# One-bank PSUM tiles in place of two-bank tiles in a fused linear-attention and token-MLP block

## The chip, the cores and the metric

The kernel runs on one core of one Trainium2 chip. The time is the device time of the execution in microseconds (us), the median of several runs; lower is better. Each run also has a mean granted TensorE clock, where 1.0 is full speed.

## The reference, cut to what matters

With x of 2048 rows and 576 columns, 32 heads of 18, and an MLP over the *rows* (tokens) with 4608 hidden units, the reference computes:

```
q, k, v = layernorm(x) @ wqkv                       # 576 -> 3 x 576
pq, pk  = phi(q), phi(k)                            # phi(t) = t+1 if t > 0 else exp(t); + 1e-6
kv, z   = pk^T v, sum over rows of pk               # per head: the "state"
o       = (pq kv) / (pq z + 1e-6)
h       = x + o @ wo
u       = gelu(layernorm(h)^T @ w1 + b1)            # contraction over 2048 rows
out     = h + (u @ w2 + b2)^T
```

Inputs and output are bf16; sums are taken in f32.

## The kernel before

It works on 16 tiles of 128 rows. It has three stages.

1. *Projections and state.* Each row tile is normalised, transposed on TensorE and evicted by ScalarE (ACT); K comes in two halves of 288 columns, V in two parts, and the state is accumulated over all tiles. After every four row tiles a "Q block" computes five groups of Q for 512 rows.
2. *Attention output, projection, second normalisation.* `nd` is the attention output of a row tile; it is divided on VectorE (DVE), transposed by a DMA into `oT`, and projected into `at`. ScalarE copies `at` to `h` with a sum and squares it with a sum; GpSimd (POOL) writes the normalised `hn`. The attention outputs run LOOK tiles ahead of the projection.
3. *The MLP.* Blocks `u` and `y`, 1152 matmuls of 288 columns each.

The program uses PSUM, the memory that matmuls write to, as eight banks of 512 f32 columns. Before, it is handed out in tiles of two banks, and four such tiles exist. One is held by the state (`kvz`) during stage 1, so three rotate.

```python
    ps = ctx.enter_context(tc.tile_pool(name="ps", bufs=4, space=bass.MemoryType.PSUM))
    def acc_tile(name):
        return ps.tile([P, 2, BANK], F32, tag="acc", name=name)

        def phi_evac(ps_ap, out_ap, rows, cols):       # exp on ACT, max on DVE, + eps on POOL
            e = ...
            nc.scalar.activation(out=e, in_=ps_ap, func=ACT.Exp, bias=-1.0, scale=1.0)
            nc.vector.scalar_tensor_tensor(out=m, in0=e, scalar=1.0, in1=ps_ap, op0=ALU.min, op1=ALU.max)
            nc.gpsimd.tensor_scalar(out=out_ap, in0=m, scalar1=1.0, scalar2=PHI_EPS, ...)

        def emit_q(c):
            for g in range(NG):                        # NG = 5
                if g % 2 == 0:
                    qps = acc_tile(f"qps{c}_{g}")      # groups g and g+1 share a two-bank tile
                reg = qps[:rg, g % 2, 0:SC]
                for kt in range(KT):                   # KT = 5 matmuls of 512 columns
                    nc.tensor.matmul(reg, ...)
                phi_evac(reg, ...)                     # reads this bank before the next group is written
        ...
            # stage 2: one copy of both banks with one sum, then the square with that sum as bias
            nc.scalar.activation(out=h_sb[:, i, :]..., in_=at_ps[:, :, 0:HD], func=ACT.Identity, accum_out=hsum)
            nc.scalar.activation(out=junk, in_=h_sb[:, i, :], func=ACT.Square, bias=hsum, ..., accum_out=ssq)
```

K has the same form as Q: half 0 goes to bank 0 and is evicted by `phi_evac`, then half 1 goes to bank 1 of the same tile. The transposes of a row tile lie in the unused columns of the K tile's two banks, so the K tile is taken from the rotation already at the transposes.

## Time and profile before

The median is 427.44 us over six runs (427.01 to 428.52). The profiled run has a span of 425.8 us at a mean clock of 0.995.

| from the span's start | us |
|---|---|
| first Q block starts | 28.8 |
| starts of the four Q blocks | 28.8, 50.9, 73.2, 98.1 |
| last state matmul starts | 95.8 |
| u starts | 139.4 |
| last u matmul starts | 280.7 |
| last y matmul starts | 421.8 |

The windows view gives, for a stretch of time, each engine's busy time (with the number of instructions), then the granted clock, the share of the DMA engines and the GB/s. The kernel before, with two lines for the first two cycles of stage 1 (a Q block and four row tiles each), one for stage 2 and one for u:

```profile
core 0: us, PE busy (x) PEld busy (x) DVE busy (x) ACT busy (x) POOL busy (x), PEclk, DMA share, GB/s
28.77:50.90 22.13, 18.98 (x146) 13.19 (x145) 12.46 (x33) 11.63 (x35) 8.86 (x18) 1.00 0.37 89
50.90:73.19 22.29, 18.99 (x146) 13.19 (x145) 11.46 (x29) 11.63 (x35) 9.09 (x19) 1.00 0.00 1
...
96.00:139.40 43.40, 37.24 (x298) 27.46 (x298) 25.97 (x95) 28.33 (x69) 27.23 (x50) 0.96 0.38 62
139.40:280.80 141.40, 141.40 (x1155) 112.76 (x1155) 0.41 (x3) 27.24 (x36) 1.86 (x4) 1.00 0.56 146
```

In the MLP TensorE is busy all the time, so nothing is to be had there. In stage 1 no engine is full, and in stage 2 none either: both are chains with waits in them. The waits view (who waited, for whom, us in total, times, longest) of the kernel before, TensorE only; waits at the start of the kernel and short ones are left out:

```profile
...
PE kps L214 <- DVE m L166: 4.5, 6, 1.0
PE qps L262 <- DVE m L166: 4.4, 5, 1.4
PE at L355 <- DMA oT<-o_buf: 3.1, 6, 1.5
PE kps L227 <- DVE m L166: 2.1, 3, 0.9
...
PE bps L404 <- DMA b_raw<-in_B_b_dram: 1.8, 1, 1.8
PE vps L235 <- DVE m L166: 0.9, 4, 0.4
...
```

Four of the six lines shown wait for the same instruction: L166, the maximum in `phi_evac`. They are of two kinds. L227 is K's second half, which waits until the first half's bank has been read. L214 (the transposes) and L235 (V) open a new tile, so they wait for one of the three tiles to come free. The timeline shows how. Its columns are start, duration, engine, line, operation, out<-in, shapes, and in brackets the idle time before and what ended it. This is the third Q block before, from the timelines of TensorE and VectorE:

```profile
73.19 2.32 PE L262 MATMUL qps<-xnT,wqkv_sb 128*126 128x512 bf16 x10
75.97 1.24 PE L262 MATMUL qps<-xnT,wqkv_sb 128*126 128x512 bf16 x5 [0.17 <-DVE m L166]
78.69 2.32 PE L262 MATMUL qps<-xnT,wqkv_sb 128*72 128x512 bf16 x10 [1.37 <-DVE m L166]
...
75.23 0.69 DVE L166 SCALAR_TENSOR_TENSOR m<-e,qps 126x512 f32<-126x512 f32 x1 [2.09 <-ACT e L164]
77.95 1.29 DVE L166 SCALAR_TENSOR_TENSOR m<-e,qps 126x512 f32<-126x512 f32 x2 [2.03 <-ACT e L164]
```

Read it across the engines: the maximum that starts at 75.23 ends at 75.92, and the group that goes to the *other* bank of that tile starts at 75.97. TensorE has put a few other matmuls in between, then runs out of them. The longer wait, 1.37 us before 78.69, is of the other kind: there the fifth group (72 rows) opens a new tile, and the tile that it gets comes free only when its second half has been read too, by the first of the two maxima at 77.95. The fifth group waits 1.37 us in each of the first three Q blocks. Twenty-five matmuls that take 5.4 us back to back (25 x 0.215) are spread over 7.8 us here.

### The profile page before, as it was taken

The numbers are of one execution on the slowest core, as the hardware profiler recorded it, in microseconds if no ns is written. First come the engines' busy times: TensorE is split into PE (matmuls) and PEld (weight loads), VectorE is DVE, ScalarE is ACT, GpSimd is POOL, SyncE is SP. The second block draws the span as 40 slices with busy tenths as digits, with TensorE's granted clock in tenths as the row PEclk, the third lists the DMA queues.
The fourth block names the chain that finished last, engine by engine and source line by source line (L and its number), as shares of the span: only waits on it lengthen the run. The fifth ranks groups of instructions, "written<-read, shape, count | busy, mean of one in ns | idle before, by whom it ended". The sixth has DMA issues, their size and how long they took to land.

```text
span 425.8 us, 7334 instructions
## 1 busy us (share of the span) xinstructions
PE 393.6 (92%) x3158; PEld 303.7 (71%) x3158; DVE 88.1 (21%) x263; ACT 101.5 (24%) x235; POOL 64.9 (15%) x132
## 2 busy tenths in 40 slices
PE   2887979788988999999999999999999999999996
PEld 1554747465765777777777777777777777777774
DVE  4655554326764000000000000000100001000010
ACT  2435545452778311221221122110000000000000
POOL 3333444321778200000000000000000000000000
PEclk9999999998999999999999999999999999999999
DMA  8774000004343997473463553000927639276300
GB/s 247 227 200 97 3 0 2 0 2 48 62 77 63 264 292 189 108 187 103 128 169 100 145 152 100 0 2 15 235 71 196 158 93 236 80 185 170 81 22 21
DMA packets 92687, 48.23 MB, mean 113 GB/s; under 512 B 12528, under 2 KB 92656, under 8 KB 92656
## 3 DMA queue, kind: packets, MB, share of 16 engines
q1 hardware_dynamic: 92656, 47.78, 43.8%
q8 instruction: 24, 0.39, 0.4%
q14 instruction: 7, 0.06, 0.0%
HBM read 42.78 MB, written 2.36 MB: 106 GB/s over the span
## 4 chain that ended last, share of the span: by engine, by line
PE 80%; DVE 8%; DMA 5%; ACT 3%; issue 2%; POOL 1%; SPq 1%; DVEq 0%; ACTq 0%; POOLq 0%
PE u L419 33%; PE y L433 33%; PE qps L262 5%; DVE m L166 4%; PE at L355 3%; DMA oT<-o_buf 3%; PE kps L227 3%; ACT e L164 2%; DVE stats L189 2%; DMA x_sb<-in_A_x_dram 2%; DVE xn_buf L198 1%; PE nd L323 1%; PE vps L235 1%; POOL rstd L196 1%; PE at L352 1%
## 5 line engine op out<-in xcount | busy, mean ns | idle before, releaser
L419 PE MATMUL u<-hn_sb,w1c 128*128 128x288 bf16 x1152 | 141.5, 286 | 0.0
L433 PE MATMUL y<-gT_sb,w2c 128*128 128x288 bf16 x1152 | 141.3, 286 | 0.0
L433 PEld LDWEIGHTS <-w2c 128*128 128x128 bf16 x1152 | 112.7, 98 | 28.4
L419 PEld LDWEIGHTS <-w1c 128*128 128x128 bf16 x1152 | 112.6, 98 | 28.4
L437 DVE SCALAR_TENSOR_TENSOR o_t<-y,b_sb,h_sb 128x576 bf16<-128x576 f32 x16 | 13.1, 818 | 269.3 <-PE y L433 269.3
L422 ACT ACTIVATE gT_sb<-u,b_sb 128x576 bf16<-128x576 f32 x36 | 26.7, 742 | 113.2 <-PE u L419 113.2
L227 PE MATMUL kps<-wqkv_sb,xnT 128*128 128x288 bf16 x160 | 27.3, 295 | 3.9 <-DVE m L166 2.1
L262 PE MATMUL qps<-xnT,wqkv_sb 128*126 128x512 bf16 (+1 forms) x100 | 24.7, 393 | 4.5 <-DVE m L166 4.4
L355 PE MATMUL at<-wo_sb,oT 128*128 128x288 bf16 x160 | 24.6, 286 | 3.1 <-DMA oT<-o_buf 3.1
L235 PE MATMUL vps<-wqkv_sb,xnT 128*128 128x378 bf16 (+1 forms) x160 | 25.3, 295 | 0.9 <-DVE m L166 0.9
L262 PEld LDWEIGHTS <-wqkv_sb 128*126 128x126 bf16 (+1 forms) x100 | 13.6, 137 | 12.7 <-issue 6.1
L227 PEld LDWEIGHTS <-xnT 128*128 128x128 bf16 x160 | 15.3, 100 | 8.8 <-issue 4.6
L235 PEld LDWEIGHTS <-xnT 128*128 128x128 bf16 x160 | 15.6, 101 | 8.2 <-issue 2.7
L355 PEld LDWEIGHTS <-oT 128*128 128x128 bf16 x160 | 14.9, 98 | 8.7 <-DMA oT<-o_buf 4.6
L214 PE MATMUL kps<-ident,xn_buf 128*128 128x128 bf16 x80 | 7.6, 229 | 12.1 <-POOL hm L300 5.5
L168 POOL TENSOR_SCALAR pk_buf<-m 128x288 bf16<-128x288 f32 x32 | 13.9, 434 | 28.1 <-DVE m L166 20.3
L164 ACT ACTIVATE e<-kps 128x288 f32<-128x288 f32 x32 | 13.2, 412 | 18.9 <-PE kps L227 18.5
L166 DVE SCALAR_TENSOR_TENSOR m<-e,qps 126x512 f32<-126x512 f32 (+1 forms) x20 | 13.0, 683 | 22.4 <-ACT e L164 22.4
L164 ACT ACTIVATE e<-qps 126x512 f32<-126x512 f32 (+1 forms) x20 | 11.1, 595 | 26.3 <-PE qps L262 26.3
L166 DVE SCALAR_TENSOR_TENSOR m<-e,kps 128x288 f32<-128x288 f32 x32 | 14.3, 447 | 14.4 <-ACT e L164 14.1
L168 POOL TENSOR_SCALAR pqT_sb<-m 126x512 bf16<-126x512 f32 (+1 forms) x20 | 12.5, 623 | 29.6 <-DVE m L166 28.9
L214 PEld LDWEIGHTS <-xn_buf 128*128 128x128 bf16 x80 | 5.8, 102 | 15.1 <-DVE xn_buf L198 8.1
(63 smaller groups left out, 196.3 us busy)
## 6 DMA issues: line engine op xcount, KB each, us to landing
w1c<-in_B_w_dram SPq DMA_DIRECT2D x18, 1024.0 KB, 6.0
w2c<-in_B_w_dram SPq DMA_DIRECT2D x8, 2304.0 KB, 10.0
out_dram<-o_t SPq DMA_DIRECT2D x16, 144.0 KB, 2.0
wqkv_sb<-in_A_wqkv_dram SPq DMA_DIRECT2D x3, 576.0 KB, 5.2
x_sb<-in_A_x_dram SPq DMA_DIRECT2D x3, 576.0 KB, 8.2
wo_sb<-in_A_wo_dram SPq DMA_DIRECT2D x1, 576.0 KB
x_sb<-in_A_x_dram SPq DMA_DIRECT2D x2, 144.0 KB, 2.1
x_sb<-in_A_x_dram SPq DMA_DIRECT2D x1, 288.0 KB
```

The costliest lines, as they stand in the source:

```text
L164: nc.scalar.activation(out=e[:rows, :cols], in_=ps_ap, func=ACT.Exp, bias=-1.0, scale=1.0)
L166: nc.vector.scalar_tensor_tensor(out=m[:rows, :cols], in0=e[:rows, :cols], scalar=1.0, in1=ps_ap, op0=ALU.min, op1=ALU.max)
L168: nc.gpsimd.tensor_scalar(out=out_ap, in0=m[:rows, :cols], scalar1=1.0, scalar2=PHI_EPS, op0=ALU.mult, op1=ALU.add)
L214: nc.tensor.transpose(dst, xn[:, kt * P:(kt + 1) * P], ident)
L227: nc.tensor.matmul(kps[:, hh, 0:HD], lhsT=xnT[:, kt, ssl], rhs=wqkv_sb[:, kt, WK + hh * HD:WK + (hh + 1) * HD], start=(kt == 0), stop=(kt ...
L235: nc.tensor.matmul(vps[:, b, 0:w], lhsT=xnT[:, kt, ssl], rhs=wqkv_sb[:, kt, WV + c0:WV + c0 + w], start=(kt == 0), stop=(kt == KT - 1))
L262: nc.tensor.matmul(reg, lhsT=wqkv_sb[:, kt, WQ + g_off[g]:WQ + g_off[g] + rg], rhs=xnT[:, kt, :], start=(kt == 0), stop=(kt == KT - 1))
L355: nc.tensor.matmul(at_ps[:, hh, 0:HD], lhsT=oT[:, kt, :], rhs=wo_sb[:, kt, hh * HD:(hh + 1) * HD], start=False, stop=(kt == KT - 1))
L419: nc.tensor.matmul(acc[:, hh, 0:HD], lhsT=w1c[:, k, j * P:(j + 1) * P], rhs=hn_sb[:, k, hh * HD:(hh + 1) * HD], start=(k == 0), stop=(k == ...
L422: nc.scalar.activation(out=gT_sb[:, ft, :].rearrange("p (a b) -> p a b", a=2), in_=acc[:, :, 0:HD], func=ACT.Gelu_apprx_tanh, bias=b1_sb[: ...
L433: nc.tensor.matmul(acc[:, hh, 0:HD], lhsT=w2c[:, ft, j * P:(j + 1) * P], rhs=gT_sb[:, ft, hh * HD:(hh + 1) * HD], start=(ft == 0), stop=(f ...
L437: nc.vector.scalar_tensor_tensor(out=o_t.rearrange("p (a b) -> p a b", a=2), in0=acc[:, :, 0:HD], scalar=b2_sb[:, i:i + 1], in1=h_sb[:, i, ...
```

## The change

The change hands PSUM out in eight tiles of one bank. The state takes two and six rotate in stage 1. It is meant to end the waits that come from the two-bank tile, and it pays for that with more and smaller instructions where one instruction used to read both banks. With it come a separate tile for the five transposes (one eviction of 640 columns instead of two), LOOK 4 with five buffers instead of LOOK 3 with four, and the MLP's bias load moved to the start. The core of the diff:

```diff
-    ps = ctx.enter_context(tc.tile_pool(name="ps", bufs=4, space=bass.MemoryType.PSUM))
-    def acc_tile(name):
-        return ps.tile([P, 2, BANK], F32, tag="acc", name=name)
+    ps = ctx.enter_context(tc.tile_pool(name="ps", bufs=8, space=bass.MemoryType.PSUM))
+    def bank_tile(name):
+        return ps.tile([P, BANK], F32, tag="bank", name=name)
 ... transposes
-            nc.scalar.activation(out=xnT[:, 0:TB0, ssl], in_=tv0, func=ACT.Identity)
-            nc.scalar.activation(out=xnT[:, TB0:KT, ssl], in_=tv1, func=ACT.Identity)
+            nc.scalar.activation(out=xnT[:, :, ic * P:(ic + 1) * P], in_=tv, func=ACT.Identity)
 ... K (V and nd in the same way)
-            kps = k_tiles.pop(i)
             for hh in range(2):
+                kps = bank_tile(f"kps{i}_{hh}")
 ... Q
-                if g % 2 == 0:
-                    qps = acc_tile(f"qps{c}_{g}")
-                reg = qps[:rg, g % 2, 0:SC]
+                qps = bank_tile(f"qps{c}_{g}")
+                reg = qps[:rg, 0:SC]
 ... projection: two copies with a sum each, and an addition of the sums on VectorE
+            for hh in range(2):
+                ...
+                nc.scalar.activation(out=h_sb[:, i, hh * HD:(hh + 1) * HD], in_=at_ps[:, 0:HD],
+                                     func=ACT.Identity, accum_out=hs[:, hh:hh + 1])
-            nc.scalar.activation(out=h_sb[:, i, :]..., in_=at_ps[:, :, 0:HD], func=ACT.Identity, accum_out=hsum)
+            nc.vector.tensor_tensor(out=hsum, in0=hs[:, 0:1], in1=hs[:, 1:2], op=ALU.add)
 ... lookahead (and five o and oT buffers instead of four)
-        LOOK = 3
+        LOOK = 4
 ... MLP: gelu and the last addition in two halves each; b1, b2 loaded and transposed earlier
```

More of the change, by code (lines that the diff above doesn't have):

```diff
@@ L67 @@
     VB = D - VA
-    TB0 = 3
-    assert (BANK - HD) * 2 >= TB0 * P and (BANK - HD) * 2 >= (KT - TB0) * P
     persist = ctx.enter_context(tc.tile_pool(name="persist", bufs=1))
@@ L127 @@
         nc.sync.dma_start(wo_sb[:RLAST, KT - 1, :], A_wo[(KT - 1) * P:D, :])
+        b1_raw = pa.tile([FT, P], BF16)
+        nc.sync.dma_start(b1_raw, B_b1.rearrange("(ft p) -> ft p", p=P))
+        b2_raw = pa.tile([NS, P], BF16)
+        nc.sync.dma_start(b2_raw, B_b2.rearrange("(i p) -> i p", p=P))
         nc.vector.memset(wqkv_sb[RLAST:P, KT - 1, :], 0.0)
@@ L150 @@
             v_bufs.append(vb)
-        NOB = 4
+        NOB = 5
         o_bufs = []
@@ L169, in phi_evac @@
                                     op0=ALU.mult, op1=ALU.add)
-        kvz = acc_tile("kvz")
-        kvz_a = kvz[:, 0, :].rearrange("p (g c) -> p g c", c=P)
-        kvz_b = kvz[:, 1, 0:P]
+        kvz_at = bank_tile("kvz_a")
+        kvz_a = kvz_at.rearrange("p (g c) -> p g c", c=P)
+        kvz_bt = bank_tile("kvz_b")
+        kvz_b = kvz_bt[:, 0:P]
         def kvz_region(g, nrows, c0, c1):
@@ L180 @@
         xnT_tiles = {}
-        k_tiles = {}
         ln_norm = {}
@@ L206, in emit_tr @@
             xn = xn_bufs[i % NXB]
-            kps = acc_tile(f"kps{i}")
-            k_tiles[i] = kps
-            tv = [kps[:, b, HD:BANK].bitcast(BF16) for b in range(2)]
-            tv0 = tv[0][:, 0:TB0 * P].rearrange("p (k c) -> p k c", c=P)
-            tv1 = tv[1][:, 0:(KT - TB0) * P].rearrange("p (k c) -> p k c", c=P)
-            for kt in range(KT):
-                dst = tv0[:, kt, :] if kt < TB0 else tv1[:, kt - TB0, :]
-                nc.tensor.transpose(dst, xn[:, kt * P:(kt + 1) * P], ident)
-            ssl = slice(ic * P, (ic + 1) * P)
-            nc.scalar.activation(out=xnT[:, 0:TB0, ssl], in_=tv0, func=ACT.Identity)
-            nc.scalar.activation(out=xnT[:, TB0:KT, ssl], in_=tv1, func=ACT.Identity)
+            tps = bank_tile(f"tps{i}")
+            tv = tps.bitcast(BF16)[:, 0:KT * P].rearrange("p (k c) -> p k c", c=P)
+            for kt in range(KT):
+                nc.tensor.transpose(tv[:, kt, :], xn[:, kt * P:(kt + 1) * P], ident)
+            nc.scalar.activation(out=xnT[:, :, ic * P:(ic + 1) * P], in_=tv, func=ACT.Identity)
         def emit_kv(i):
@@ L223, in emit_kv @@
             pk_sb = pk_bufs[i % NPK]
-            kps = k_tiles.pop(i)
             for hh in range(2):
+                kps = bank_tile(f"kps{i}_{hh}")
                 for kt in range(KT):
-                    nc.tensor.matmul(kps[:, hh, 0:HD], lhsT=xnT[:, kt, ssl],
+                    nc.tensor.matmul(kps[:, 0:HD], lhsT=xnT[:, kt, ssl],
                                      rhs=wqkv_sb[:, kt, WK + hh * HD:WK + (hh + 1) * HD],
                                      start=(kt == 0), stop=(kt == KT - 1))
-                phi_evac(kps[:, hh, 0:HD], pk_sb[:, hh * HD:(hh + 1) * HD], P, HD)
+                phi_evac(kps[:, 0:HD], pk_sb[:, hh * HD:(hh + 1) * HD], P, HD)
             v_sb = v_bufs[i % NVB]
-            vps = acc_tile(f"vps{i}")
             for b, (c0, w) in enumerate(((0, VA), (VA, VB))):
+                vps = bank_tile(f"vps{i}_{b}")
                 for kt in range(KT):
-                    nc.tensor.matmul(vps[:, b, 0:w], lhsT=xnT[:, kt, ssl],
+                    nc.tensor.matmul(vps[:, 0:w], lhsT=xnT[:, kt, ssl],
                                      rhs=wqkv_sb[:, kt, WV + c0:WV + c0 + w],
                                      start=(kt == 0), stop=(kt == KT - 1))
-            nc.scalar.activation(out=v_sb[:, 0:NPB, 0:RG],
-                                 in_=vps[:, 0, 0:VA].rearrange("p (g c) -> p g c", c=RG), func=ACT.Identity)
-            nc.scalar.activation(out=v_sb[:, NPB, 0:RG], in_=vps[:, 1, 0:RG], func=ACT.Identity)
-            nc.scalar.activation(out=v_sb[:, NPB + 1, 0:VB - RG], in_=vps[:, 1, RG:VB], func=ACT.Identity)
+                if b == 0:
+                    nc.scalar.activation(out=v_sb[:, 0:NPB, 0:RG],
+                                         in_=vps[:, 0:VA].rearrange("p (g c) -> p g c", c=RG), func=ACT.Identity)
+                else:
+                    nc.scalar.activation(out=v_sb[:, NPB, 0:RG], in_=vps[:, 0:RG], func=ACT.Identity)
+                    nc.scalar.activation(out=v_sb[:, NPB + 1, 0:VB - RG], in_=vps[:, RG:VB], func=ACT.Identity)
         def emit_kvacc(i):
@@ L254, in emit_q @@
             xnT = xnT_tiles[c]
-            qps = None
             for g in range(NG):
                 rg = g_rows[g]
-                if g % 2 == 0:
-                    qps = acc_tile(f"qps{c}_{g}")
-                reg = qps[:rg, g % 2, 0:SC]
+                qps = bank_tile(f"qps{c}_{g}")
+                reg = qps[:rg, 0:SC]
                 for kt in range(KT):
@@ L286 @@
         emit_kvacc(NS - 1)
+        bps = bank_tile("bps")
+        bpv = bps.bitcast(BF16)
+        nc.tensor.transpose(bpv[:, 0:FT], b1_raw, ident[:FT, :FT])
+        nc.tensor.transpose(bpv[:, 512:512 + NS], b2_raw, ident[:NS, :NS])
+        nc.vector.tensor_copy(out=b1_sb, in_=bpv[:, 0:FT])
+        nc.vector.tensor_copy(out=b2_sb, in_=bpv[:, 512:512 + NS])
         bm = pa.tile([P, GH, Dh], F32)
@@ L318, in emit_nd @@
         def emit_nd(i):
-            nd = acc_tile(f"nd{i}")
-            for g in range(NG):
-                rg = g_rows[g]
-                b, sl = divmod(g, NPB)
-                nc.tensor.matmul(nd[:, b, sl * NDW:sl * NDW + RG + GH],
-                                 lhsT=pqT_sb[:rg + 1, g, i * P:(i + 1) * P],
-                                 rhs=R_sb[:rg + 1, g, 0:RG + GH], start=True, stop=True)
             rden = small.tile([P, NG, GH], F32, tag="rden")
             o_sb = o_bufs[i % NOB]
+            nds = []
             for b in range(2):
@@ L330, in emit_nd @@
                 g0 = b * NPB
-                ndv = nd[:, b, 0:ns_ * NDW].rearrange("p (s c) -> p s c", c=NDW)
-                nc.vector.reciprocal(out=rden[:, g0:g0 + ns_, :], in_=ndv[:, :, RG:RG + GH])
+                nd = bank_tile(f"nd{i}_{b}")
+                for sl in range(ns_):
+                    g = g0 + sl
+                    rg = g_rows[g]
+                    nc.tensor.matmul(nd[:, sl * NDW:sl * NDW + RG + GH],
+                                     lhsT=pqT_sb[:rg + 1, g, i * P:(i + 1) * P],
+                                     rhs=R_sb[:rg + 1, g, 0:RG + GH], start=True, stop=True)
+                nds.append(nd)
             for b in range(2):
@@ L335, in emit_nd @@
                 g0 = b * NPB
-                ndv = nd[:, b, 0:ns_ * NDW].rearrange("p (s c) -> p s c", c=NDW)
+                ndv = nds[b][:, 0:ns_ * NDW].rearrange("p (s c) -> p s c", c=NDW)
+                nc.vector.reciprocal(out=rden[:, g0:g0 + ns_, :], in_=ndv[:, :, RG:RG + GH])
                 nc.vector.tensor_tensor(
@@ L341, in emit_nd @@
                     op=ALU.mult)
-            oT = work.tile([P, KT, P], BF16, tag="oT", name=f"oT{i}", bufs=4)
+            oT = work.tile([P, KT, P], BF16, tag="oT", name=f"oT{i}", bufs=5)
             nc.sync.dma_start_transpose(out=oT, in_=o_sb)
@@ L349, in emit_wo_h @@
             oT = oT_tiles.pop(i)
-            at_ps = acc_tile(f"at{i}")
+            hs = small.tile([P, 2], F32, tag="hs")
             for hh in range(2):
-                nc.tensor.matmul(at_ps[:, hh, 0:HD], lhsT=ident, rhs=x_sb[:, i, hh * HD:(hh + 1) * HD],
+                at_ps = bank_tile(f"at{i}_{hh}")
+                nc.tensor.matmul(at_ps[:, 0:HD], lhsT=ident, rhs=x_sb[:, i, hh * HD:(hh + 1) * HD],
                                  start=True, stop=False)
                 for kt in range(KT):
-                    nc.tensor.matmul(at_ps[:, hh, 0:HD], lhsT=oT[:, kt, :],
+                    nc.tensor.matmul(at_ps[:, 0:HD], lhsT=oT[:, kt, :],
                                      rhs=wo_sb[:, kt, hh * HD:(hh + 1) * HD],
                                      start=False, stop=(kt == KT - 1))
+                nc.scalar.activation(out=h_sb[:, i, hh * HD:(hh + 1) * HD], in_=at_ps[:, 0:HD],
+                                     func=ACT.Identity, accum_out=hs[:, hh:hh + 1])
             hsum = small.tile([P, 1], F32, tag="hsum")
-            nc.scalar.activation(out=h_sb[:, i, :].rearrange("p (a b) -> p a b", a=2), in_=at_ps[:, :, 0:HD],
-                                 func=ACT.Identity, accum_out=hsum)
+            nc.vector.tensor_tensor(out=hsum, in0=hs[:, 0:1], in1=hs[:, 1:2], op=ALU.add)
             junk = work.tile([P, D], BF16, tag="junk", bufs=2)
@@ L396 @@
         outp = bctx.enter_context(tc.tile_pool(name="outp", bufs=3))
-        b1_raw = pb.tile([FT, P], BF16)
-        nc.sync.dma_start(b1_raw, B_b1.rearrange("(ft p) -> ft p", p=P))
-        b2_raw = pb.tile([NS, P], BF16)
-        nc.sync.dma_start(b2_raw, B_b2.rearrange("(i p) -> i p", p=P))
-        bps = acc_tile("bps")
-        bpv = [bps[:, b, :].bitcast(BF16) for b in range(2)]
-        nc.tensor.transpose(bpv[0][:, 0:FT], b1_raw, ident[:FT, :FT])
-        nc.tensor.transpose(bpv[1][:, 0:NS], b2_raw, ident[:NS, :NS])
-        nc.vector.tensor_copy(out=b1_sb, in_=bpv[0][:, 0:FT])
-        nc.vector.tensor_copy(out=b2_sb, in_=bpv[1][:, 0:NS])
         gT_sb = pb.tile([P, FT, D], BF16)
@@ L415 @@
                 ft = fc * (FCW // P) + j
-                acc = acc_tile(f"u{ft}")
+                accs = [bank_tile(f"u{ft}_{hh}") for hh in range(2)]
                 for k in range(NS):
                     for hh in range(2):
-                        nc.tensor.matmul(acc[:, hh, 0:HD], lhsT=w1c[:, k, j * P:(j + 1) * P],
+                        nc.tensor.matmul(accs[hh][:, 0:HD], lhsT=w1c[:, k, j * P:(j + 1) * P],
                                          rhs=hn_sb[:, k, hh * HD:(hh + 1) * HD],
                                          start=(k == 0), stop=(k == NS - 1))
-                nc.scalar.activation(out=gT_sb[:, ft, :].rearrange("p (a b) -> p a b", a=2), in_=acc[:, :, 0:HD],
-                                     func=ACT.Gelu_apprx_tanh, bias=b1_sb[:, ft:ft + 1], scale=1.0)
+                for hh in range(2):
+                    nc.scalar.activation(out=gT_sb[:, ft, hh * HD:(hh + 1) * HD], in_=accs[hh][:, 0:HD],
+                                         func=ACT.Gelu_apprx_tanh, bias=b1_sb[:, ft:ft + 1], scale=1.0)
         w2v = B_w2.rearrange("(ft p) s -> p ft s", p=P)
@@ L429 @@
                 i = sc * (SCW // P) + j
-                acc = acc_tile(f"y{i}")
+                accs = [bank_tile(f"y{i}_{hh}") for hh in range(2)]
                 for ft in range(FT):
                     for hh in range(2):
-                        nc.tensor.matmul(acc[:, hh, 0:HD], lhsT=w2c[:, ft, j * P:(j + 1) * P],
+                        nc.tensor.matmul(accs[hh][:, 0:HD], lhsT=w2c[:, ft, j * P:(j + 1) * P],
                                          rhs=gT_sb[:, ft, hh * HD:(hh + 1) * HD],
@@ L436 @@
                 o_t = outp.tile([P, D], BF16, tag="o_t")
-                nc.vector.scalar_tensor_tensor(
-                    out=o_t.rearrange("p (a b) -> p a b", a=2), in0=acc[:, :, 0:HD], scalar=b2_sb[:, i:i + 1],
-                    in1=h_sb[:, i, :].rearrange("p (a b) -> p a b", a=2), op0=ALU.add, op1=ALU.add)
+                for hh in range(2):
+                    nc.vector.scalar_tensor_tensor(
+                        out=o_t[:, hh * HD:(hh + 1) * HD], in0=accs[hh][:, 0:HD], scalar=b2_sb[:, i:i + 1],
+                        in1=h_sb[:, i, hh * HD:(hh + 1) * HD], op0=ALU.add, op1=ALU.add)
                 nc.sync.dma_start(out2[i * P:(i + 1) * P, :], o_t)
```

## The prediction

> **What bounds the kernel now.** Three stages, by the windows view. (1) 0 to 96 us: projections and state. (2) 96 to 139.5 us: attention output, projection, second normalisation. (3) 139.5 to 422 us: two MLP matmul blocks of 141 us each with TensorE never waiting; 3.7 us of tail follow. Stage 3 is bound by TensorE and keeps its 1152 + 1152 matmuls at 123 ns, so only stages 1 and 2 (139.5 us) can move.
>
> Stage 1: from the timeline's start-to-start spacing, one row tile costs TensorE about 3.0 us (5 transposes 0.28, ten 288-column matmuls 1.22, V 1.23, state 0.28), one Q block 5.4 us (25 x 0.215). Four tiles plus a Q block are 17.4 us; the trace takes 22.1 to 22.8 us. The waits view names the reason: TensorE waits for the DVE maximum (L166) before kps, qps and vps. The instruction order shows why: each two-bank tile is tracked as one, so the second half's matmuls wait until exp (0.41 to 0.60 us) and maximum (0.45 to 0.69 us) of the first half have read the other bank; only three such tiles rotate.
>
> **What the change does there.** One-bank tiles end the false wait, six banks rotate, and TensorE's new order is plain program order. A bank is needed again five groups later, about 2.7 us, against about 1.4 us of exp + maximum. The two transpose evictions (0.49 + 0.38) become one of 640 columns: 0.72 us by the Trainium skill ("ScalarE: Activation LUTs", What ACT_TABLE_LOAD costs: 186 ns + 0.833 ns per column; the trace agrees, 493 ns at 384). ACT needs about 2.6 and DVE about 2.4 us a tile, both under 3.0. I estimate the first Q block at 24 us (now 28.8; start-up stays held by loads, a slow TensorE and the normalisation chain) and 18.3 us a cycle: the state ends near 80.5 us instead of 96, a gain of about 15.5 us.
>
> **What it costs.** Stage 2: ACT now spends about 1.65 us a tile (copy 0.55, accumulator read 0.22, square 0.68, read 0.2), close to TensorE's 1.77, and tiles pass at about 1.85 us. Afterwards copy and accumulator read come twice (0.53 each), then ACT waits for the new DVE add (about 0.25 with hops), then square 0.88: 2.2 us a tile in order, so ACT becomes the bound. Q3 is no longer interleaved: projection begins about 10 us after the state (6.6 now). hn of tile 15 comes about 47.3 us after the state; u's last k step needs it. Before, u's end lay 185 us after the state; afterwards about 47.3 + 140.9 = 188.2. Loss about 3 us, in spite of the early bias load, which takes away a 1.8 us wait. LOOK 4 and the fifth buffers barely matter once ACT bounds. Gelu in halves (72 x about 0.5 us) stays hidden. The last output addition gains about 0.1 us.
>
> **Predicted.** 427.4 - 15.5 + 3.2 = about 415.3 us; range 410.5 to 421.5. Faster by over 2%: 0.78; within 2%: 0.21; slower: 0.01.
>
> **Right if:** waits of kps, qps, vps on L166 nearly vanish from the waits view; Q blocks lie 18 to 19 us apart; kvz ends at 79 to 83 us; in stage 2 the square waits for the hsum add, tiles pass every 2.1 to 2.4 us; u and y stay 141 us each.
>
> **Wrong if:** six banks or the DVE order (normalisation between maxima) still stall TensorE, cycles 20 us or more; or ACT hides the add, and stage 2 shortens too; or start-up, held by loads, gives nothing.

## The result

The changed kernel takes 403.67 us (median of eight runs, 403.05 to 405.0), the kernel before 427.21 us in the same rounds (16 runs). The ratio is 0.9453, with a 95% interval from 0.9436 to 0.9471: it is 5.5% faster. Among runs at a clock of 0.998 or more the means are 426.3 (runs of before beside the experiments) and 403.7. Here and below a ratio is the mean time of one kernel's fast runs over that of the other's in the same rounds, so it is not quite the ratio of the quoted medians. The direction was right; the time lies below the predicted range (410.5 to 421.5), since the gain is 23.7 us and not 12.

| us | before | after |
|---|---|---|
| span of the profiled run | 425.8 | 402.1 |
| starts of the four Q blocks | 28.8, 50.9, 73.2, 98.1 | 23.6, 41.6, 59.0, 79.8 |
| last state matmul starts | 95.8 | 76.6 |
| first projection matmul starts | 102.6 | 85.2 |
| u starts, last u matmul starts | 139.4, 280.7 | 113.6, 256.6 |
| last state matmul to last u matmul | 184.9 | 180.0 |
| last u matmul to the end of the span | 145.1 | 145.5 |

The gain of 23.7 us is thus 19.2 in stage 1 (95.8 - 76.6), 4.9 from there to the end of u, and -0.4 after it. Two reservations: the profiles of x6 and x13 below, whose stage 1 has the code of before, have the last state matmul at 95.0 and 94.5, so about 1 us of the 19.2 may be scatter of one profile; and some 1.4 to 1.7 of the 4.9 are a dip of the clock in the profile of before ("The clock dip" below). The windows view after, the same four stretches:

```profile
23.61:41.59 17.98, 17.59 (x149) 13.04 (x147) 14.72 (x43) 11.88 (x30) 9.45 (x19) 1.00 0.68 177
41.59:59.02 17.43, 17.43 (x149) 13.05 (x147) 11.84 (x30) 11.88 (x30) 10.15 (x21) 1.00 0.00 1
...
76.70:113.60 36.90, 35.05 (x302) 26.95 (x300) 27.55 (x109) 26.65 (x92) 24.37 (x44) 1.00 0.40 73
113.60:256.80 143.20, 141.49 (x1155) 112.75 (x1153) 0.73 (x5) 35.26 (x81) 4.94 (x10) 1.00 0.54 144
```

In the second cycle TensorE is busy for 17.43 of 17.43 us: stage 1 is now bound by TensorE once it has started. In u, 1.7 us of the 143.2 are idle. The waits view after, TensorE, again without the start:

```profile
...
PE u L415 <- POOL hn_sb L383: 1.7, 2, 1.4
PE kps L224 <- DVE m L169: 1.0, 2, 0.5
PE at L361 <- DMA oT<-o_buf: 1.0, 2, 0.7
...
PE qps L259 <- DVE m L169: 0.4, 1, 0.4
```

The maximum is L169 now. Waits for it fell from 11.9 us (4.5 + 4.4 + 2.1 + 0.9) to 1.4 us, and the wait for `oT` from 3.1 to 1.0. The largest wait past the start is a new one: u waits for the last normalised tiles. And the third Q block after, TensorE and the first two maxima:

```profile
59.02 5.56 PE L259 MATMUL qps<-xnT,wqkv_sb 128*126 128x512 bf16 x25
...
61.00 0.69 DVE L169 SCALAR_TENSOR_TENSOR m<-e,qps 126x512 f32<-126x512 f32 x1 [2.39 <-ACT e L167]
62.08 0.69 DVE L169 SCALAR_TENSOR_TENSOR m<-e,qps 126x512 f32<-126x512 f32 x1 [0.39 <-ACT e L167]
```

All 25 matmuls stand in one line without a wait, while exponentials and maxima run alongside them.

### The profile page after: what moved, and what is told of

The parts are those of the page before. It is cut to its first block, busy times and chain, and to the rows that moved or that the text cites. A ratio compares the mean times of both kernels' runs of the same rounds, so it can differ in the third digit from the quotient of the medians.

```text
span 402.1 us, 7403 instructions
## 1 busy us (share of the span) xinstructions
PE 385.3 (96%) x3158; PEld 302.3 (75%) x3158; DVE 92.5 (23%) x296; ACT 109.0 (27%) x287; POOL 65.3 (16%) x132
## 4 chain that ended last, share of the span: by engine, by line
PE 84%; ACT 6%; DVE 4%; POOL 2%; DMA 1%; issue 1%; SPq 1%; POOLq 0%; DVEq 0%
PE y L430 35%; PE u L415 34%; PE qps L259 5%; PE kps L224 4%; PE vps L232 4%; ACT junk L370 3%; ACT h_sb L364 3%; DMA x_sb<-in_A_x_dram 1%; DVE stats L192 1%; POOL rstd L199 1%; PE kvz_a L247 1%; PE tps L213 1%; DVE xn_buf L201 1%; DVE hsum L367 1%; DVE m L169 0%
## 5 line engine op out<-in xcount | busy, mean ns | idle before, releaser
L435 DVE SCALAR_TENSOR_TENSOR o_t<-y,b_sb,h_sb 128x288 bf16<-128x288 f32 x32 | 15.1, 513 | 267.0 <-PE y L430 267.0
L419 ACT ACTIVATE gT_sb<-u,b_sb 128x288 bf16<-128x288 f32 x72 | 32.1, 498 | 107.7 <-PE u L415 107.7
L224 PE MATMUL kps<-wqkv_sb,xnT 128*128 128x288 bf16 x160 | 23.8, 296 | 1.0 <-DVE m L169 1.0
L259 PE MATMUL qps<-xnT,wqkv_sb 128*126 128x512 bf16 (+1 forms) x100 | 22.4, 379 | 0.4 <-DVE m L169 0.4
L232 PE MATMUL vps<-wqkv_sb,xnT 128*128 128x378 bf16 (+1 forms) x160 | 22.7, 289 | 0.0
L167 ACT ACTIVATE e<-qps 126x512 f32<-126x512 f32 (+1 forms) x20 | 11.9, 597 | 15.7 <-PE qps L259 14.4
L169 DVE SCALAR_TENSOR_TENSOR m<-e,kps 128x288 f32<-128x288 f32 x32 | 14.0, 444 | 6.6 <-ACT e L167 6.6
L169 DVE SCALAR_TENSOR_TENSOR m<-e,qps 126x512 f32<-126x512 f32 (+1 forms) x20 | 13.4, 682 | 7.5 <-ACT e L167 7.4
L213 PE MATMUL tps<-ident,xn_buf 128*128 128x128 bf16 x80 | 7.6, 230 | 7.7 <-POOL hm L304 5.5
L342 DVE TENSOR_TENSOR o_buf<-nd,rden 128x378 bf16<-128x378 f32 (+1 forms) x32 | 13.9, 473 | 0.0
```

The lines of the kernel that those rows point to most:

```text
L167: nc.scalar.activation(out=e[:rows, :cols], in_=ps_ap, func=ACT.Exp, bias=-1.0, scale=1.0)
L169: nc.vector.scalar_tensor_tensor(out=m[:rows, :cols], in0=e[:rows, :cols], scalar=1.0, in1=ps_ap, op0=ALU.min, op1=ALU.max)
L224: nc.tensor.matmul(kps[:, 0:HD], lhsT=xnT[:, kt, ssl], rhs=wqkv_sb[:, kt, WK + hh * HD:WK + (hh + 1) * HD], start=(kt == 0), stop=(kt == K ...
L232: nc.tensor.matmul(vps[:, 0:w], lhsT=xnT[:, kt, ssl], rhs=wqkv_sb[:, kt, WV + c0:WV + c0 + w], start=(kt == 0), stop=(kt == KT - 1))
L259: nc.tensor.matmul(reg, lhsT=wqkv_sb[:, kt, WQ + g_off[g]:WQ + g_off[g] + rg], rhs=xnT[:, kt, :], start=(kt == 0), stop=(kt == KT - 1))
L342: nc.vector.tensor_tensor(out=o_sb[:, g0 * RG:(g0 + ns_) * RG].rearrange("p (s j e) -> p s j e", s=ns_, j=GH), in0=ndv[:, :, 0:RG].rearran ...
```

## The experiments

All fourteen kernels gave correct results. "Before" had medians of 426.75 to 427.64 us beside them.

### Stage 1: what was it about the two-bank tiles?

Four readings were possible. The wait is on TensorE alone, for the second half of a tile (then it helps to give TensorE both halves first). Or the tile serialises its readers too. Or fewer tiles means less capacity. Or a tile is held too long, since the K tile also holds the transposes.

**x1_hoist_kq.** The kernel before, with both halves' matmuls emitted before either eviction. Tiles and pool stay.

```diff
 ... K: the evictions leave the loop that has the matmuls
+            for hh in range(2):
                 phi_evac(kps[:, hh, 0:HD], ...)
 ... Q: five groups in pairs
+                for g in pair:
+                    for kt in range(KT): nc.tensor.matmul(qps[:rg, g % 2, 0:SC], ...)
+                for g in pair:
+                    phi_evac(qps[:rg, g % 2, 0:SC], ...)
```

> The kernel before with its two-bank tiles and three rotating tiles, but both halves' matmuls of K and both groups' matmuls of a Q pair are emitted ahead of both evictions. If the false wait inside a two-bank tile is what stage 1 lost (theory A), most of the gain of 19 us comes without one-bank tiles: 410 to 417 us, Q blocks 18 to 20 us apart, state ended by 80 to 86 us. If the finer rotation of one-bank tiles is what counts (rival B), it stays at 423 to 428 us.

Measured: 419.15 us, ratio 0.9816 (0.9781 to 0.985). The last state matmul starts at 88.7 instead of 95.8, and a cycle takes 20.3 us (48.27 to 68.55). It lies between the two ranges, and neither reading holds by itself: stage 1 becomes 7.1 us shorter, of 19.2. In the waits view TensorE's waits for the other half of a tile are gone, and 4.8 us of waits for a free tile (L214, V and the first group of a Q tile, on the maximum) are left. These lines of its timeline show what took the place of the old wait:

```profile
60.57 0.44 DVE L166 SCALAR_TENSOR_TENSOR m<-e,kps 128x288 f32<-128x288 f32 x1
61.04 0.41 ACT L164 ACTIVATE e<-kps 128x288 f32<-128x288 f32 x1 [1.04 <-DVE m L166]
61.48 0.46 DVE L166 SCALAR_TENSOR_TENSOR m<-e,kps 128x288 f32<-128x288 f32 x1 [0.17 <-ACT e L164]
61.99 0.44 PE L214 MATMUL kps<-ident,xn_buf 128*128 128x128 bf16 x5 [0.62 <-DVE m L166]
```

The exponential of half 1 only *reads* its bank, and so does the maximum of half 0 in the other bank; still the exponential starts at 61.04, just after the maximum that ran from 60.57 to 61.01. It is not a wait for one of the three buffers of `e`, since the maximum at 60.57 is that of the exponential just before. Two readers on different engines are put one after the other, as long as they read the same tile. ScalarE's waits view of this run sums it:

```profile
ACT e L164 <- DVE m L166: 20.5, 21, 2.8
```

By the built program's semaphores all 21 wait for a maximum of the other half of the same tile. So the tile is one object in both ways: TensorE's write waits for the other half's readers, and readers wait for each other; and since the halves are read one after the other, the tile comes free late. The Trainium skill, "PSUM — Partial Sum Buffer", section "PSUM bank collisions raise a hardware error", says that two engines must not be in the same bank and the same quadrant of 32 partitions at once, reads against reads included, and gives the rule to guard by bank. That asks for no guard between two banks. The changed kernel agrees: with one-bank tiles its results are correct with no such wait in its trace (exponentials wait for a maximum twice, 1.4 us, both times for a buffer of `e`). The waits of before are therefore made by the tile, not by the chip.

**x1q_hoist_q.** The same for Q alone (the second half of the diff above).

> As x1_hoist_kq, but only the Q pairs are hoisted. Theory A: the Q block shrinks from about 9 us to 6 or 7 us, four blocks, so 416 to 421 us, about half of the gain. Rival B: 425 us or more.

Measured: 421.64 us, ratio 0.9871 (0.9836 to 0.9906); the last state matmul starts at 90.5. This is just above the expected 421. Most of the hoist's gain, about 5.5 of 8 us, is Q's.

**x2_six_banks.** The changed kernel with `bufs=6` instead of 8: four banks rotate in stage 1, fewer than the six banks in three tiles of before.

> The changed kernel with six banks in place of eight, so four rotating ones beside the state's two: less PSUM in rotation than the three two-bank tiles of the kernel before had. Theory A: most of the gain stays, 404 to 410 us, TensorE waiting for banks a few us in all. Rival B (the number of slots in rotation counts): 415 us or more.

Measured: 408.18 us, ratio 0.955 (0.9516 to 0.9584). Q blocks start at 26.15, 43.73, 61.23: the cycle is still 17.5 us. With less PSUM in rotation than before, the cycle is as short as after. Capacity is not the cause. The number of tiles is not settled to the last, as four rotate here and three before: a run with three one-bank tiles was not made. Of the 4.5 us that it loses, the profile has 2.2 at the start-up of stage 1 (state at 78.8) and 2.6 from the state to the end of u (182.6 instead of 180.0); about 1.7 of the latter are a clock dip in this profile (0.82, 0.50 and 0.83 from 82 to 88). The one run at a clock of 1.0 took 406.73, 3.0 more than the change.

**x8_transposes_in_k_banks.** The changed kernel, but the transposes lie in the K halves' banks again and are evicted in two pieces, as before.

```diff
-            tps = bank_tile(f"tps{i}")
-            tv = tps.bitcast(BF16)[:, 0:KT * P]...
+            kps = [bank_tile(f"kps{i}_{hh}") for hh in range(2)]
+            tv = [kps[hh][:, HD:BANK].bitcast(BF16) for hh in range(2)]   # 3 transposes in one, 2 in the other
```

> The changed kernel with one-bank tiles throughout, but the five transposes go back into the banks of the K halves (three beside half 0, two beside half 1, two evictions), so these banks are held from the transposes of a tile until its K maxima, as before. x1_hoist_kq left 12 us of stage 1's 19 us unexplained: either (C) the long hold of K's tiles by the transposes in a pool of few slots, or (D) the waits between engines within a two-bank tile that hoisting does not remove (exp of half 1 waited for the maximum of half 0, 10.8 us in x1). Under C this run loses most of that again: 410 us or more, the state ended after 83 us. Under D it stays within 3 us of the changed kernel: 404 to 407 us, the state ended by 80 us.

Measured: 406.50 us, ratio 0.9509 (0.9484 to 0.9534). Q blocks at 26.35, 44.03, 61.65, so the cycle is 17.65 us. The long hold costs about 2.4 us in all (405.93 and 406.39 at a clock of 0.999 or 1.0, against 403.7) and next to nothing per cycle. In the profile 2.7 us are lost before the first Q block, but a clock dip lies there too (0.59 and 0.56 from 18 to 22). What remains as the cause of the 22 us cycle is the two-bank tile as one object: halves that wait for each other, and a tile that comes free only as a whole.

**x10_warm_start.** The first ten K matmuls take 2.4 us, against 1.22 later. The Trainium skill, "TensorE: Matmul & The Clock Gate", section "What's actually happening", says that TensorE starts at half clock and is released by activity. So here TensorE gets 44 idle-time transposes of the identity before its first real work.

> The changed kernel with 44 transposes of the identity ahead of and between the first real transposes, in TensorE's idle time before 8.5 us. In the changed kernel the first ten K matmuls took 2.4 us and the first ten V ones 1.7, against 1.22 each later. Theory: TensorE runs slowly because it has just been idle, and start-up is on the chain: 1 to 1.7 us gained, 402.0 to 402.8. Rival: start-up is held by the normalisation chain on DVE and POOL, and the TensorE time gained is waited away: within 0.4 us of 403.7.

Measured: 405.26 us, ratio 0.9491 (0.9464 to 0.9519): 1.6 us slower than the change, or 1.2 at a clock of 0.999 or 1.0 (404.63 and 405.10). This is outside both ranges. The first K matmuls did take 1.22 us, which agrees with the page. But the scheduler also put the maxima of K tile 0 behind the next tile's normalisation, and the state ended later (77.9). The time that TensorE won it spent waiting for VectorE (2.7 us for `m` before K, against 1.0). In this order VectorE's chain holds start-up; since the edit changed that order too, what the clock alone costs there is not shown.

### Stage 2: why did it not become longer?

**x6_split_copy_before.** The kernel before with the split copy and the added addition alone.

```diff
-            nc.scalar.activation(out=h_sb[:, i, :]..., in_=at_ps[:, :, 0:HD], func=ACT.Identity, accum_out=hsum)
+            for hh in range(2):
+                nc.scalar.activation(out=h_sb[:, i, hh * HD:(hh + 1) * HD], in_=at_ps[:, hh, 0:HD],
+                                     func=ACT.Identity, accum_out=hs[:, hh:hh + 1])
+            nc.vector.tensor_tensor(out=hsum, in0=hs[:, 0:1], in1=hs[:, 1:2], op=ALU.add)
```

> The kernel before with only the copy of the projection split in two, its two accumulator reads and the added DVE sum; nothing else. If ScalarE's longer chain (1.94 us a tile measured after the change, 1.54 at least before) costs what it seems to, the 16 tiles of stage 2 pass at 1.95 us instead of 1.85 and the time grows by 1 to 4 us. If ScalarE's chain is hidden behind TensorE and the DMA transposes, it grows by less than 0.7 us.

Measured: 428.90 us, ratio 1.0048 (1.0009 to 1.0087). It costs 1 to 2 us: 2.0 by the ratio, 1.0 in the profile (185.9 from the state to the last u matmul instead of 184.9). The loss that the prediction feared is real and smaller.

**x4_look3.** The changed kernel with LOOK 3 and four buffers.

> The changed kernel with look-ahead 3 and four o and oT buffers, as before. If stage 2 gained because the transposing DMAs are started one tile earlier (TensorE's waits for oT fell from 3.1 to 1.0 us), the time rises by 2 to 4 us and those waits return. If ScalarE's chain and TensorE bound the stage and the look-ahead is spare, it rises by less than 0.7 us.

Measured: 405.52 us, ratio 0.9495 (0.9475 to 0.9516). The lookahead is worth 1.8 us after the change, just under the expected 2; the projection waits 2.5 us for `oT` instead of 1.0.

**x13_before_look4.** The kernel before with LOOK 4 and five buffers, nothing else.

```diff
-        NOB = 4
+        NOB = 5
-            oT = work.tile([P, KT, P], BF16, tag="oT", name=f"oT{i}", bufs=4)
+            oT = work.tile([P, KT, P], BF16, tag="oT", name=f"oT{i}", bufs=5)
-        LOOK = 3
+        LOOK = 4
```

> The kernel before with LOOK 4 and five output buffers, nothing else. If the lookahead shortens the second stage by itself (it was worth 1.8 us in the changed kernel): 425.0 to 426.0 us, a ratio near 0.996. If it does so only with one-bank tiles, because a two-bank tile kept for one more tile takes a slot from the rotation: 426.8 us or more, a ratio of 1.0 or above.

Measured: 423.81 us, ratio 0.9938 (0.9892 to 0.9983). This is more than expected. Its runs fall into groups by clock, so like is best compared with like: three runs at a clock of 0.999 or 1.0 took 422.27, 422.43 and 422.84, and the sixteen runs of before at 0.998 or more have a mean of 426.3: about 3.8 us. (Its other three, at 0.987 to 0.996, took 424.78 to 427.57.) In the profiles about 2.7 of this lie in stage 2 (180.5 us from the last state matmul to the last u matmul, against 184.9 less a clock dip of 1.7) and 1.3 before the end of the state, where the edit changes next to nothing. The profile says where it comes from. These are lines of POOL's timeline, the writes of `hn`, first of the kernel before:

```profile
121.95 0.83 POOL L376 TENSOR_SCALAR hn_sb<-h_sb,r,cc 128x576 bf16<-128x576 f32 x1
123.90 0.82 POOL L376 TENSOR_SCALAR hn_sb<-h_sb,r,cc 128x576 bf16<-128x576 f32 x1
127.33 0.82 POOL L376 TENSOR_SCALAR hn_sb<-h_sb,r,cc 128x576 bf16<-128x576 f32 x1
```

then of x13_before_look4:

```profile
121.88 0.82 POOL L376 TENSOR_SCALAR hn_sb<-h_sb,r,cc 128x576 bf16<-128x576 f32 x1
123.68 0.82 POOL L376 TENSOR_SCALAR hn_sb<-h_sb,r,cc 128x576 bf16<-128x576 f32 x1
125.48 0.82 POOL L376 TENSOR_SCALAR hn_sb<-h_sb,r,cc 128x576 bf16<-128x576 f32 x1
```

The tiles' pace is 1.81 us in both (POOL's three instructions per tile), but before it has holes: 3.43 us instead of 1.81 after 123.90. Just ahead of that hole the kernel before has this wait of TensorE, for the transpose of a row tile:

```profile
122.70 0.79 PE L355 MATMUL at<-wo_sb,oT 128*128 128x288 bf16 x5 [1.49 <-DMA oT<-o_buf]
```

In the waits view the 3.1 us of waiting for `oT` by DMA are gone from x13. So before, POOL set the pace of stage 2, and late DMA transposes made the holes in it.

**x12_stage2_two_bank.** The changed kernel, but from the first projection tile on the tiles of stage 2 are two-bank tiles in a pool of four, with the single copy and no addition. Stage 1, the last Q block and LOOK 4 stay as changed.

```diff
+        close_pool("ps")           # eight one-bank tiles
+        open_pool("ps2", 4)        # four two-bank tiles: at, and nd of tiles 4 to 15
         for i in range(NS):
             emit_wo_h(i)
 ... and before u:
+        close_pool("ps2")
+        open_pool("ps", 8)
```

> The changed kernel with the second stage's tiles as before from the first projection tile on: attention outputs of tiles 4 to 15 and all projections in four rotating two-bank tiles, one copy with one sum, no addition; the first stage, the last Q block in one-bank tiles, LOOK 4 and five buffers stay. From the end of the state to the last u matmul the trace has 184.9 us before and 180.0 us after. Theory P (the stage became shorter because of its one-bank tiles): this run gives most of it back, 183 to 185 us from the state to the last u matmul, 406 to 408 us in all. Theory Q (it became shorter because the last Q block now runs in one piece at full clock and because of LOOK 4, in spite of the split copy, whose price in the kernel before was about 1.7 us): this run is the faster one, 178 to 179 us from the state to the last u matmul, 402 to 402.6 us in all.

Measured: 403.70 us, ratio 0.945 (0.9423 to 0.9477), and 180.1 us from the last state matmul to the last u matmul: the same as the change. Theory P is refuted, as two-bank tiles with the single copy give nothing back on the net. Theory Q's 402 us was not reached either. The switch of pools brought waits of its own (the first projection waits 1.5 us for the last Q maximum, u 1.1 us for the last copy), so how much the single copy would save is not settled by this run.

**x3_late_bias.** The changed kernel with the bias load and its transposes back at the start of the MLP.

> The changed kernel with the bias load put back to where it was, at the start of the MLP. Theory: u's last k steps wait for hn of the last tiles (until 119.3 us in the trace) and not for the biases, so the early load is worth under 0.5 us: 403.5 to 404.3. Rival: the 1.8 us that TensorE waited for the bias load before were on the path, and come back: 405.3 to 405.8.

Measured: 403.99 us, ratio 0.9468 (0.9444 to 0.9493). The early bias is worth 0 to 0.6 us: u starts at 115.5 instead of 113.6, but then has less to wait for, since `hn` is what it needs.

### Stage 2: can it be made shorter still?

**x5_square_late.** The changed kernel with the square of tile i emitted between the two copies of tile i+1, to hide ScalarE's wait for the addition.

> The changed kernel with the square of tile i emitted between the two copies of tile i+1, so that ScalarE does not stand still for the DVE sum. Theory: ScalarE's chain of 1.94 us a tile makes hn of the last tile late (5.7 us after the projection's last matmul); at 1.65 us a tile it keeps up with TensorE's 1.77, and u's wait for hn of 1.7 us mostly goes: 402.0 to 403.0 us. Rival (the latency of the last tile's own chain ends the stage): no change, within 0.5 us.

Measured: 403.94 us, ratio 0.9453. This run tells nothing: the scheduler put the square back, and ScalarE's built order is the same as before the edit.

**x5b_square_forced.** The same, with an ordering edge from that copy to the square.

```diff
+                if hh == 0 and i > 0:
+                    emit_sq(i - 1, cp)          # cp: the copy just emitted
...
+            order_after(sq, after_copy)
```

> x5_square_late again, as it should have been: its built order of ScalarE had not changed (the scheduler put the square back ahead of the next copy). Now an ordering edge keeps the square of tile i behind the first copy of tile i+1. Theory: the chain of 1.94 us a tile falls to about 1.65, below TensorE's 1.77, hn of the last tile comes about 1 to 1.5 us earlier, 402.2 to 403.0 us. Rival (the last tile's own latency ends the stage): within 0.4 us of 403.7.

Measured: 404.70 us, ratio 0.945 (0.9421 to 0.9479). Two runs at a clock of 0.999 to 1.0 took 402.62 and 402.78, three at 0.994 or 0.995 took 404.7 to 405.0. The runs of the change at a clock of 0.998 or more have a mean of 403.7, its one run at 0.996 took 405.0, so the gain over the change is between 0.2 and 1 us, and over all runs it is unclear. The timeline of POOL shows why it is no more:

```profile
111.86 0.82 POOL L391 TENSOR_SCALAR hn_sb<-h_sb,r,cc 128x576 bf16<-128x576 f32 x1
112.65 0.55 POOL L388 TENSOR_TENSOR r<-w,neg_half 128x1 f32<-128x1 f32 x1
113.30 0.27 POOL L390 TENSOR_SCALAR cc<-hsum,r 128x1 f32<-128x1 f32 x1
113.67 0.82 POOL L391 TENSOR_SCALAR hn_sb<-h_sb,r,cc 128x576 bf16<-128x576 f32 x1
```

Freed of ScalarE, the tiles pass every 1.81 us, and now POOL is full. u still waits 1.9 us for `hn`.

**x9_two_u_tiles.** The changed kernel, but the first two tiles of u first take row tiles 0 to 12 of both, then 13 to 15 of both.

```diff
+            split = NS - 3 if fc == 0 else NS
+            spans = [(j, 0, split) for j in range(FCW // P)]
+            if split < NS:
+                spans += [(j, split, NS) for j in range(FCW // P)]
+            for j, k0, k1 in spans:
+                for k in range(k0, k1):
```

> The changed kernel with the first two u tiles sharing the wait: k steps 0 to 12 of both, then 13 to 15 of both, so that TensorE has 3 us more work before it needs hn of the last row tiles. Theory: TensorE's 1.7 us of waiting for hn at the start of u go, 401.8 to 402.4 us. Rival (TensorE was held by something else there, or the gap moves): 403.3 or more.

Measured: 401.65 us (401.42 to 403.25), ratio 0.9404 (0.9376 to 0.9432). The wait for `hn` is gone from the waits view. It beats both kernels, by slightly more than expected.

**x11_both_mends.** x9_two_u_tiles and x5b_square_forced together.

> The changed kernel with both mends of stage 2 together: the first two u tiles take k 0 to 12 of both before k 13 to 15 (as in x9_two_u_tiles), and the square is forced behind the next tile's first copy (as in x5b_square_forced). Theory (the two act on different waits: the first hides u's wait for the last normalised tiles, the second shortens ScalarE's tile by the wait for the addition, and in x5b's profile the projection phase was 0.9 us shorter): 400.5 to 401.2 us, u starts about 0.9 us sooner after the state than in x9. Rival (TensorE's projection phase is set by POOL's chain or by the copies, or the wait for hn comes back because the square is late): 401.3 to 401.9 us, as x9_two_u_tiles alone, or worse.

Measured: 401.07 us (400.92 to 402.17), ratio 0.9386 (0.9356 to 0.9416), the fastest kernel. It is in the theory's range. The difference from x9 is small: at a clock of 0.999 or 1.0 the means are 401.14 (four runs) and 401.60 (four runs), and the intervals of the two ratios overlap. Of the detail expected, u 0.9 us sooner after the state, the profile shows nothing: u starts 37.4 us after the last state matmul, against 37.0 in x9, but this profiled run had the clock dip described below and x9's had not.

## Why the prediction was right or wrong

**Right.** TensorE's waits on the maximum almost vanish (11.9 to 1.4 us). The cause was in the main the one named, a two-bank tile tracked as one: x2 and x8 rule out PSUM's size and the long hold, and x1 shows that giving TensorE both halves first is not enough. But the wait that the prediction put first, the second half's matmuls behind the first half's readers, was only about 2.4 of TensorE's 11.9 us; the rest was for one of three tiles to come free. How much the number of tiles counts, apart from each being freed as a whole, stays open. The first Q block starts at 23.6 (predicted 24). u and y stay at 141 us of matmuls each. The square does wait for the addition (3.9 us in 14 waits). The early bias is worth little.

**Stage 1, mis-sized by 3.7 us.** The prediction said "18.3 us a cycle: the state ends near 80.5 us". The step that failed is the allowance over TensorE's own work of 17.4 us. The cycles took 17.98, 17.43 and 17.7 us: once the rotation is free, hardly a stall is left, and the state ended at 76.7. This is 1.8 us of the 3.7, and the first Q block came 0.4 sooner. The other 1.6 are in the sum itself: 24 and three cycles of 18.3 make 78.9 and not 80.5, and the prediction does not say what the rest was for.

**Stage 2, wrong in sign.** The prediction said "Loss about 3 us"; the profiles show a gain of 4.9 us. Three terms of its sum failed.

The largest is "2.2 us a tile in order, so ACT becomes the bound". The mechanism was right: `hn` passes every 1.94 us after the change, as ScalarE's tiles do, and every 1.81 in x5b, where ScalarE no longer waits for the addition. The size was wrong. ScalarE's timeline before, one tile:

```profile
115.32 0.65 ACT L359 ACTIVATE h_sb<-at 128x576 f32<-128x576 f32 x1 [0.90 <-PE nd L323]
115.86 0.20 ACT L359 ACTIVATION_READ_ACCUMULATOR h_sb<-at 128x1 f32 x1
116.09 0.78 ACT L363 ACTIVATE junk<-h_sb,hsum 128x576 bf16<-128x576 f32 x1
```

and after:

```profile
103.70 0.39 ACT L364 ACTIVATE h_sb<-at 128x288 f32<-128x288 f32 x1
103.99 0.19 ACT L364 ACTIVATION_READ_ACCUMULATOR h_sb<-at 128x1 f32 x1
104.08 0.40 ACT L364 ACTIVATE h_sb<-at 128x288 f32<-128x288 f32 x1
104.38 0.20 ACT L364 ACTIVATION_READ_ACCUMULATOR h_sb<-at 128x1 f32 x1
104.87 0.78 ACT L370 ACTIVATE junk<-h_sb,hsum 128x576 bf16<-128x576 f32 x1 [0.30 <-DVE hsum L367]
...
105.64 0.39 ACT L364 ACTIVATE h_sb<-at 128x288 f32<-128x288 f32 x1
```

A copy and its accumulator read were predicted at 0.53 us; from start to start they take 0.38 (103.70 to 104.08). The next instruction starts 0.09 us after the read does. I had taken the read as 0.22 us from the kernel before, where the next instruction, the square, needs the read's result and starts 0.23 us after it (115.86 to 116.09). In the new order the next instruction often does not. The same holds for the square with its read: predicted 0.88, it takes 0.77 (104.87 to 105.64). A tile takes 1.94 us (103.70 to 105.64): 0.26 less than predicted, 4.2 us over 16 tiles. The Trainium skill, "ScalarE: Activation LUTs", section "What ACT_TABLE_LOAD costs", the very place that I cited for the durations, also says that back-to-back ACTIVATEs overlap by about 93 ns. The trace agrees (a copy of 0.39 us whose read starts 0.29 us after it), and I did not use it.

Second, "projection begins about 10 us after the state": it began 8.6 us after (76.6 to 85.2). Third, "47.3 + 140.9": nearly all of u was put after the last normalised tile. In the trace that tile's write starts at 118.4, when TensorE has already done about 4 us of u's matmuls (it started at 113.6 and waited 1.7), and y follows 138.4 us later. The three terms are 4.2, 1.4 and 2.5 us, which make the 8.1 us between a loss of 3.2 and a gain of 4.9. The base had a fault too: the 185 us of before that the prediction counted from hold the clock dip described below, so against a run of before without it the gain is nearer 3.3 us. The prediction's own "wrong if" had this outcome, "stage 2 shortens too", but for another reason: ScalarE did wait for the addition.

**"LOOK 4 and the fifth buffers barely matter once ACT bounds" failed too.** They are worth 1.8 us after the change (x4) and about 2.7 us of stage 2 in the kernel before (x13). The prediction read the pace of before ("tiles pass at about 1.85 us") but not its holes, which were waits for DMA transposes.

**Where stage 2's gain comes from.** x13 alone has 180.5 us from the last state matmul to the last u matmul, x12 180.1, the change 180.0, the kernel before 184.9. So the lookahead (about 2.7 us), together with a clock dip that the profile of before had and the others had not (about 1.7 us, next paragraph), covers nearly all of the difference between the profiles of before and of x13, and x13 is within 0.5 us of the change. One-bank tiles are not needed for it, and the split copy costs 1 to 2 us that something else in the change gives back; I did not isolate what. The last Q block in one piece is a candidate, and that is only argued.

**The clock dip.** The page of before was of an execution in which TensorE's granted clock fell just after the state. Windows view of the kernel before:

```profile
96.00:98.00 2.00, 1.45 (x14) 1.28 (x15) 1.76 (x10) 0.00 (x0) 0.00 (x0) 0.80 0.00 0
98.00:100.00 2.00, 2.00 (x8) 1.21 (x7) 1.85 (x7) 0.00 (x0) 0.00 (x0) 0.50 0.00 0
100.00:102.00 2.00, 2.00 (x10) 1.09 (x9) 2.00 (x7) 0.60 (x1) 0.00 (x0) 0.85 0.42 82
```

The clock is given third from the end: 0.80, 0.50, 0.85. That is half speed for about 3.4 us (0.4 + 1.0 + 0.3 us lost, doubled), and 1.7 us lost make 0.4% of the span, just the 0.995 or 0.996 of such runs. Of 47 executions of before beside the experiments, 31 had a clock of 0.996 or less (mean 427.7) and 16 had 0.998 or more (mean 426.3). Such dips come and go in the other kernels too (in x11's profile one lies in the last Q block, in x1's one lies later, after 125 us, and one of the change's nine runs had a clock of 0.996). They were seen less often after the change and in the kernels made from it (17 of 51 runs of these had 0.996 or less); whether the change makes them rarer was not tested. They are part of the difference between two profiles. A comparison of one profile with one other can hold 1.4 us of it.

## What to carry to other kernels

Allocate PSUM in the unit in which it is consumed: where two banks are written and read as separate halves by several engines, one tile over both made each half wait for the other's readers here, and readers on different engines for each other, and came free only as a whole; moving the matmuls ahead got back only 7 of the 19 us. When costing the instructions of one engine, measure start to start in a place where the next instruction is as independent as it will be in the new order. And look at the holes in a pipeline's pace, not only at its pace: a lookahead one deeper removed waits for DMA that no engine's busy time showed.

## What the Trainium skill lacked or had wrong

- "PSUM — Partial Sum Buffer" gives the rule to guard by bank, but does not say that a tile over several banks can be guarded as a whole. In x1_hoist_kq that made ScalarE's exponentials wait 20.5 us (21 times) for maxima of the tile's other half, readers of different banks; with one-bank tiles a cycle of stage 1 went from 22.3 to 17.4 us.
- "ScalarE: Activation LUTs", "What ACT_TABLE_LOAD costs", gives the cost of an ACTIVATE and the overlap of 93 ns, but nothing for reading the accumulator after it. Here that read shows as 0.19 to 0.21 us, of which 0.09 us delay an independent next ACTIVATE. Its formula fits the 640-column eviction (719 ns by the formula, 691 to 710 measured) and is somewhat high for the 288-column copy (426 ns by the formula, 388 to 412 measured).
- "TensorE: Matmul & The Clock Gate", "What's actually happening", has the clock fall after an idle window of about 3.4 us, and "HAM oscillation — how this bites in real kernels" puts the rule as no idle gaps above that. In the profile of before it fell to 0.50 where TensorE's longest gap in the 4 us ahead was 0.57 us, and by the mean clock something of this size happened in 31 of 47 executions. The length of the dip, about 3.4 us, and the half clock agree with the page. Its section "A second HAM failure mode: psum-queue depth-cycling" does describe dips from short gaps, for another kernel and without a size of gap.
